# Decay columns for one more head pair, masks built on the core, and three moved steps in a fused attention and feed-forward kernel

## The chip, the core and the metric

The kernel runs on one core of a Trainium2 chip. The metric is the device time of one execution in microseconds (us). Seven runs of the kernel before gave a median of 367.82 us, from 362.78 to 372.94 us. One more execution was profiled: it took 362.79 us, of which 361.1 us lie between its first and its last instruction (the span). All times of single steps below come from that profiled execution and count from the start of its span.

## What is computed

Attention with a decay bias over 8 batches of 8 heads (576 positions, 64 numbers per head), followed by a feed-forward block with a hard-swish on the joined heads.

```python
scores = q @ k.T / sqrt(64)                       # per batch and head
cum    = cumsum(max(s, 0), axis=-1)
bias   = -(cum[:, None] - cum[None, :])
scores = where(upper triangle, -1e9, scores + min(bias, 0))
attn   = softmax(scores)
x      = (attn @ v), heads joined: 4608 x 512
h      = x @ w_in                                  # 512 -> 2048
out    = (h * clip(h + 3, 0, 6) / 6) @ w_out       # 2048 -> 512
```

## The kernel before

**Tiles.** The 64 heads are handled as 32 pairs. For a pair, q and k come from DRAM as f32 tiles of 128 positions (`qkf`), are cast to f16 by GpSimd, and are transposed by TensorE, so that the 64 head numbers lie on partitions 0 to 63 of a slot of `qkT` (three slots, used in turn: pair p lies in slot p % 3). Partitions 64 to 127 of a slot hold what is added to the scores by the same matmul: rows 64 to 67 the decay (for k the running sum in three f16 pieces, for q its negative, and ones opposite), rows 68 to 127 a coarse causal mask in steps of 10 positions. A score matmul over all 128 partitions so gives product, decay and mask at once. ScalarE takes the exponential into `Pm`, GpSimd clears the part above the diagonal (line 350), TensorE multiplies with `v` (line 425, `attend`), VectorE divides (lines 435 and 437), and a transpose puts the result into `xT`. The feed-forward block works on 9 blocks of 512 positions: `m1` (line 495) makes 16 pieces per block, each finished by ScalarE (line 505) and VectorE (line 506), and `m2` (line 540) makes the output.

**Four ways to put decay and mask into a slot.** Pairs 0 to 3 (`FIRST = 4`): the tile `x0` holds q or k cast to f16 together with 4 decay columns, which `first_columns` (line 742) makes with matmuls from a running sum over 64 positions each; `turn_first` (line 768 on) transposes q and k separately, 68 columns wide, and the eviction (line 781) writes rows 0 to 67. The mask rows of the three slots are copied once from a constant tile `amask` (`mask_part`, line 180; `mask_rows`, line 173). The fine mask is a third operand: a matmul of the identity `ident` with `tri`. Pairs 4 to 9: `transpose_group` (line 297) transposes q and k together; the decay rows come from DRAM, where `store_aug` put them after `decay_scan` and `decay_rows`, and `load_aug` reads them back. Pairs 10 to 31: one DMA transposes the tile `xb`, whose upper half holds the mask columns; these come from a constant in DRAM (`load_columns`, line 233), and GpSimd copies them into both buffers of `xb` (`copy_columns`, line 237).

**Order of work.** The order on each engine is that of the program text; nothing is moved by a scheduler. SyncE (SP) issues nearly all loads, in program order, and a load that has to wait holds up those behind it. GpSimd (POOL) issues the loads of `w_in` and `w_out` on a queue of their own (q0; SP's is q1). The stages are: a start (to some 9 us) in which TensorE runs filler matmuls on a zero tile (`keep_warm`); pairs 0 to 3 in halves of a head (to some 28 us); the first feed-forward block; pair 4 with pieces of it between; then `second_pair(p)` for pairs 5 to 8 (to some 75 us), in which one `m2` step is put in at fixed places; then `weave`, which spreads the attention of the remaining pairs among the `m1` and `m2` tasks by their weights. PSUM has eight banks: scores use the ring S (0, 1, 2), `m1` and `m2` mostly M (3, 4) and Y (5), the attention result 6 and 7.

Of the kernel before, what the change touches and what calls it, by code (L numbers as in the profile page):

```python
# [10 lines left out]
F16 = mybir.dt.float16  # L11
AF = mybir.ActivationFunctionType
ALU = mybir.AluOpType
# [3 lines left out]
def kernel(  # L17
# [10 lines left out]
    nc = tc.nc  # L28
# [40 lines left out]
    tri_np = np.where(np.arange(128)[None, :] < np.arange(128)[:, None], -65504.0, 0.0)  # L69
    idtri_dram = nc.inline_tensor(  # L70
        np.concatenate([np.eye(128), tri_np], axis=1).astype(np.float16), name="idtri"
    )

    NG = 72
    g = np.arange(NG)
# [13 lines left out]
    amask_np[1, 4:64] = np.where(gran[None, :] < rows[:, None], -16384.0, 0.0)  # L89
    MW = SEQ + 64  # L90
    amask_dram = nc.inline_tensor(
        np.ascontiguousarray(amask_np[:, :, np.arange(MW) % SEQ]), name="amask"
    )

    row = np.arange(W2).reshape(NTR, 128).T % SEQ
# [5 lines left out]

    FIRST = 4
    NA = 2 * (PTD - FIRST)
    aug_dram = nc.dram_tensor("aug_scratch", (2, 4, NA * SEQ), F16, kind="Internal").ap()
# [22 lines left out]
    XW = 68  # L127
    x0 = gT2[:, 1].rearrange("p f t -> p (f t)")[:, 0:FIRST * NTR * 2 * XW].rearrange(
        "p (a t i c) -> p a t i c", a=FIRST, t=NTR, i=2
    )  # L130

    amask = work.tile([128, 2, MW], F16, tag="amask", bufs=1)
    s_first = work.tile([NG, 64], F32, tag="s_first", bufs=1)
# [25 lines left out]

    nc.gpsimd.memset(warm, 0.0)  # L160
    nc.gpsimd.memset(x0[:, :, :, 0, D:D + 3], 1.0)
    nc.gpsimd.memset(x0[:, :, :, 1, D + 3:D + 4], 1.0)
    nc.gpsimd.memset(kT[:, :, W2:W2 + 64], 0.0)
    nc.gpsimd.memset(aug[:, 0, 0:3, :], 1.0)
    nc.gpsimd.memset(aug[:, 1, 3, :], 1.0)

    def more_pads():
        nc.gpsimd.memset(v_f[64:128, :, :, 4, :], 0.0)
        nc.gpsimd.memset(v_h[:, :, :, :, D:VW], 1.0)
        nc.gpsimd.memset(Pm[:, :, 1600:PW], 1.0)  # L170

    def mask_rows(sl, i, copy):
        copy(
            out=(kT, qT)[i][64:128, sl, 0:W2].rearrange("p (h t) -> p h t", h=2),
            in_=amask[64:128, i:i + 1, 0:SEQ].to_broadcast([64, 2, SEQ]),
        )

    def mask_part(sl, i, part, copy):
        c0, c1 = ((0, MW), (64, SEQ))[part]
        copy(  # L180
            out=(kT, qT)[i][64:128, sl, (0, MW)[part]:(MW, W2)[part]],
            in_=amask[64:128, i, c0:c1],
        )

# [32 lines left out]
    def load_aug(p, eng):  # L217
        sl = p % NS
        c0 = (p - FIRST) * W2
# [77 lines left out]
    def transpose_group(p, g):  # L297
        t0, t1 = ((0, 5), (5, 9))[g]
        n = (t1 - t0) * 128
        pT = f16(bank("S") if p == FIRST else PS[:, 3, :], n)  # L300
# [209 lines left out]
    def m1(n, f):  # L510
        if n == 0 and f < 8:
            ph = bank("A")
        elif n == 1 and f % 3 == 0:
            ph = bank("Y")
        elif n == 0 and f % 3 == 2:
            ph = bank("Y")
        elif n >= B - 1 and f % 2:
            ph = bank("S")
        else:
            ph = bank()  # L520
        m1_sum(n, f, ph, range(KC))
        m1_act(n, f, ph)
# [61 lines left out]
    def store_aug(eng):  # L584
        eng.dma_start(
            out=aug_dram.rearrange("i r (h t) -> h (i r) t", t=SEQ),
            in_=aug[2 * FIRST:2 * FIRST + NA].rearrange("h i r t -> h (i r) t"),
        )

    def load_pair(p):  # L590
        load_qk(p, nc.sync)
        load_v(p, nc.sync)
# [46 lines left out]
    def second_pair(p, fill):  # L639
# [6 lines left out]

        load_pair(p + 3)
        run(s0[:1])
        if first:
# [24 lines left out]
        if first:  # L674
            cast_qk(p + 1)
        cast_v(p + 1)
        if PTD <= p + 2:
            cast_columns(p + 2)
            transpose_dma(p + 2)
# [62 lines left out]
    def first_columns():  # L742
# [7 lines left out]
        for half in range(2):  # L750
# [7 lines left out]
            )  # L758
        c3 = cT.rearrange("p (a t) -> p a t", a=FIRST)
        r3 = rest.rearrange("p (a t) -> p a t", a=FIRST)  # L760
        hi, mid, lo = (x0[:, :, :, 1, D + j] for j in range(3))
# [23 lines left out]
    qk_tile(0)  # L785
    nc.sync.dma_start(out=s_first, in_=s[0].rearrange("h (c t) -> (h c) t", t=64))
    load_part(0, 0, 0, 5, A)
    A.dma_start(out=sums, in_=sums_dram.ap())
    load_part(0, 1, 0, 5, nc.sync)
    A.dma_start(out=idtri, in_=idtri_dram.ap())  # L790
    nc.sync.dma_start(out=amask[64:128], in_=amask_dram.ap().rearrange("i p t -> p i t"))
    load_part(0, 0, 5, 9, nc.sync)
# [8 lines left out]
    cast_first(0, 0, 0, 5, A.copy)  # L801
    cast_first(0, 1, 0, 5, G.tensor_copy)
    first_columns()
    mask_part(0, 1, 0, A.copy)
    mask_part(0, 0, 0, G.tensor_copy)
    keep_warm(4)
# [3 lines left out]
    cast_first(0, 1, 5, 9, G.tensor_copy)  # L810
    for i in range(2):
        mask_part(0, i, 1, V.tensor_copy)
    for i in range(2):
        mask_rows(1, i, V.tensor_copy)
    keep_warm(3)
    qk_f.pop(0)
    more_pads()
    for i in range(2):
        mask_rows(2, i, V.tensor_copy)

    def cast_pair(p):
        G.tensor_copy(out=x0[:, p, :, :, 0:D], in_=qk_f.pop(p))

    for hd in range(2 * FIRST):
        p, odd = hd // 2, hd % 2
        scores_half(hd, 0)
        if hd == 0:
            turn_first(0, 0, 5, 9, 6, V.tensor_copy)
            turn_first(0, 1, 5, 9, 7, V.tensor_copy)
        if not odd:  # L830
            if p == 0:
# [7 lines left out]
            if p == 1:  # L839
                nc.sync.dma_start(out=s_sb, in_=s.rearrange("b h t -> (b h) t"))  # L840
                load_v(3, nc.sync)
                load_qk(4, nc.sync)
            if p == 2:
                load_v(4, nc.sync)
                load_columns()
            if p == 3:
# [39 lines left out]
    m2_of = {n: m2_tasks(n) for n in range(NBLK)}  # L886
    run(transposes(FIRST))
    run(m1_0[10:12])
# [50 lines left out]
```

## Time and profile before

| | |
|---|---|
| median of 7 runs | 367.82 us |
| profiled execution, its span | 362.79 us, 361.1 us |
| TensorE (PE) busy | 350.6 us, 97% of the span |
| ScalarE (ACT), VectorE (DVE), GpSimd (POOL) busy | 209.0, 183.7, 152.7 us |
| clock granted to TensorE | 1.0 throughout |
| read from and written to DRAM | 37.54 MB, 9.55 MB |

The numbers are read as follows. A row of the timeline gives the start, the length, the engine (SPq and the like are the engines' queues of DMA issues), the line of the program, the operation and its tiles, how many instructions are merged, and in brackets the idle time before the row and what ended it. A row of waits gives who waited for whom, the sum, the number and the longest. A row of a DMA queue gives packets, megabytes and the share of the time of 16 DMA engines. PE is busy for 97% of the span, so what a change can take away from the end is mostly PE's idle time and PE's own work; a busy PE includes the filler matmuls of the start.

### The profile page before, as it was taken

What the parts mean: (1) busy time and instruction counts of PE and PEld (TensorE: products, weight loads), DVE (VectorE), ACT (ScalarE), POOL (GpSimd) and SP (SyncE); (2) the same over time, 40 slices, a digit from 0 to 9 for tenths busy, and PEclk for the clock granted to TensorE, in tenths of its full rate; (3) what the DMA queues carried; (4) which work ended last, traced back from release to release, by engine and by line L of the source; (5) the groups of instructions that cost most, each with busy time, mean ns of one, the idle gap of its engine ahead of it and who ended that gap; (6) DMA issues with size and microseconds to landing.
All of it is one profiled execution on the core that took longest, in us unless ns stands there. A gap on an engine that the chain in (4) does not pass through costs nothing.

```text
span 361.1 us, 7692 instructions
## 1 busy us (share of the span) xinstructions
PE 350.6 (97%) x2855; PEld 204.4 (57%) x2855; DVE 183.7 (51%) x309; ACT 209.0 (58%) x391; POOL 152.7 (42%) x375
## 2 busy tenths in 40 slices
PE   7899989999899999999999999999999999999996
PEld 3775546656555555555555555555555544544444
DVE  3776847656624554355535442545254636554431
ACT  3575637659936774677557764776477705543310
POOL 6659538755545454445544544555444200000000
PEclk9999999999999999999999999999999999999999
DMA  8999999999999899888988999999946110010012
GB/s 189 220 195 222 214 204 223 220 207 218 200 211 210 198 194 206 214 169 197 218 210 172 207 203 218 183 209 199 231 91 115 49 59 30 11 49 30 31 58 87
DMA packets 185586, 59.33 MB, mean 164 GB/s; under 512 B 177588, under 2 KB 180316, under 8 KB 185548
## 3 DMA queue, kind: packets, MB, share of 16 engines
q1 hardware_dynamic: 181832, 54.24, 67.2%
q0 software_dynamic: 2688, 4.19, 6.4%
q10 hardware_dynamic: 1028, 0.40, 0.4%
q8 instruction: 22, 0.36, 0.4%
q14 instruction: 16, 0.13, 0.1%
HBM read 37.54 MB, written 9.55 MB: 130 GB/s over the span
## 4 chain that ended last, share of the span: by engine, by line
PE 80%; DMA 6%; POOL 5%; ACT 3%; issue 2%; DVE 2%; SPq 0%; ACTq 0%; POOLq 0%; DVEq 0%
PE PS L540 31%; PE PS L495 29%; PE PS L337 8%; PE PS L425 6%; DMA qkf<-in_k_dram 4%; POOL t L227 2%; POOL Pm L350 1%; ACT Pm L345 1%; DMA aug_scratch<-aug 1%; PE PS L775 1%; PE PS L403 1%; ACT trl L505 1%; DVE gT L506 1%; PE PS L560 1%; DMA sums<-sums 1%
## 5 line engine op out<-in xcount | busy, mean ns | idle before, releaser
L506 DVE SCALAR_TENSOR_TENSOR gT<-trl,PS 128x512 f16<-128x512 f32 x144 | 98.2, 686 | 106.2 <-ACT trl L505 106.1
L495 PE MATMUL PS<-xT,w_in 128*128 128x512 f16 x576 | 143.7, 379 | 0.8 <-DVE gT L506 0.7
L505 ACT ACTIVATE trl<-PS,bias 128x512 f32<-128x512 f32 x144 | 99.0, 692 | 74.9 <-PE PS L495 73.0
L540 PE MATMUL PS<-w_out_sb,gT 128*128 128x512 f16 x560 | 138.5, 379 | 1.2 <-DVE gT L506 1.2
L345 ACT ACTIVATE Pm<-PS 128x384 f16<-128x384 f32 x224 | 103.1, 507 | 49.9 <-PE PS L337 48.6
L350 POOL TENSOR_SCALAR_AFFINE_SELECT Pm<-Pm 128x256 f16<-128x256 f16 x224 | 68.5, 307 | 118.2 <-ACT Pm L345 110.0
L495 PEld LDWEIGHTS <-w_in 128*128 128x128 f16 x576 | 61.3, 114 | 45.0 <-issue 2.0
L540 PEld LDWEIGHTS <-gT 128*128 128x128 f16 x560 | 51.4, 98 | 50.0 <-issue 1.7
L337 PE MATMUL PS<-qkT 128*128 128x256 f16 x392 | 63.2, 261 | 0.1
L337 PEld LDWEIGHTS <-qkT 128*128 128x128 f16 x392 | 36.2, 98 | 30.2 <-DVE qkT L308 1.2
L425 PEld LDWEIGHTS <-Pm 128*128 128x128 f16 x960 | 38.7, 97 | 10.9 <-DVE xs L437 0.7
L425 PE MATMUL PS<-v_h,Pm 128*128 128x65 f16 x960 | 41.9, 193 | 0.5 <-DVE xs L437 0.5
L549 DVE TENSOR_SCALAR osb<-PS 128x512 f32<-128x512 f32 x35 | 24.1, 688 | 32.9 <-PE PS L540 29.8
L437 DVE TENSOR_TENSOR xs<-PS,r 128x640 f16<-128x640 f32 x32 | 26.4, 825 | 1.1
L275 POOL CAST xb<-qkf 128x1152 f16<-128x1152 f32 x22 | 25.2, 1147 | 0.0
L290 POOL CAST v_h<-v_f 128x640 f16<-128x640 f32 x32 | 23.3, 729 | 1.5 <-DMA v_f<-in_v_dram 1.4
L409 ACT ACTIVATE Pm<-PS 128x896 f16<-128x896 f32 (+1 forms) x16 | 13.2, 836 | 5.7 <-PE PS L403 5.6
L308 DVE COPY qkT<-PS 64x640 f16<-64x640 f16 (+1 forms) x24 | 10.9, 454 | 9.2 <-PE PS L293 9.0
L435 DVE RECIPROCAL r<-PS 128x10 f32<-128x10 f32 x32 | 6.9, 216 | 8.0 <-PE PS L425 7.8
L403 PE MATMUL PS<-qkT 128*128 128x64 f16 (+4 forms) x48 | 9.6, 287 | 1.1 <-DVE qkT L781 1.0
L471 DVE COPY xT<-PS 128x576 f16<-128x576 f16 x14 | 6.4, 455 | 5.8 <-PE PS L463 4.5
L570 ACT ACTIVATE osb<-PS 128x256 f32<-128x256 f32 x1 | 0.4, 383 | 13.2 <-PE PS L560 13.2
(67 smaller groups left out, 126.0 us busy)
## 6 DMA issues: line engine op xcount, KB each, us to landing
out_dram<-osb SPq DMA_DIRECT2D x35, 256.0 KB, 2.3
qkf<-in_q_dram SPq DMA_DIRECT2D x31, 288.0 KB, 3.6
qkf<-in_k_dram SPq DMA_DIRECT2D x31, 288.0 KB, 3.7
v_f<-in_v_dram SPq DMA_DIRECT2D x64, 128.0 KB, 3.4
w_in<-in_moe_w_in_dram POOLq DMA_DIRECT2D x4, 512.0 KB, 12.6
w_out_sb<-in_moe_w_out_dram POOLq DMA_DIRECT2D x4, 512.0 KB, 13.4
v_f<-in_v_dram SPq DMA_DIRECT2D x32, 32.0 KB, 3.3
qkT<-xb SPq DMA_TRANSPOSE x22, 4.7
```

Of the source, the lines that this page charges most:

```text
L275: nc.gpsimd.tensor_copy(out=x.rearrange("p (i t) c -> p t i c", i=2)[:, :, :, 0:D], in_=qk_f.pop(p))
L290: nc.gpsimd.tensor_copy(out=v_h[:, sl, :, :, 0:D], in_=v_f[:, sl])
L337: nc.tensor.matmul(out=S[:, c:c + hi - lo], lhsT=kT[:, sl, off + 128 * kt:off + 128 * (kt + 1)], rhs=qT[:, sl, off + lo:off + hi], start=( ...
L345: nc.scalar.activation(out=P[:, p0:p0 + n], in_=S[:, 0:n], func=AF.Exp, scale=0.125, bias=0.0)
L350: nc.gpsimd.affine_select(out=view, in_=view, pattern=pattern, compare_op=ALU.is_ge, fill=0.0, base=0, channel_multiplier=-1,)
L425: nc.tensor.matmul(out=O[:, hh, qt * VW:qt * VW + D + 1], lhsT=P[:, c:c + 128], rhs=v_h[:, sl, hh, kt, 0:D + 1], start=(qt == 0), stop=(qt ...
L437: nc.vector.tensor_tensor(out=xs.rearrange("p t h d -> p h t d"), in0=Ov[:, :, :, 0:D], in1=r.to_broadcast([128, 2, 5, D]), op=ALU.mult,)
L495: nc.tensor.matmul(out=ph, lhsT=w_in_t[f // 4][:, kc, f % 4, :], rhs=xT[:, kc, n * 512:(n + 1) * 512], start=(kc == 0), stop=(kc == KC - 1),)
L505: nc.scalar.activation(out=trl, in_=ph, func=AF.Relu, bias=bias3[:, 0:1], scale=1.0)
L506: nc.vector.scalar_tensor_tensor(out=gT2[:, n % 2, f, :], in0=trl, scalar=6.0, in1=ph, op0=ALU.min, op1=ALU.mult)
L540: nc.tensor.matmul(out=po, lhsT=gT2[:, n % 2, f, t4 * 128:(t4 + 1) * 128], rhs=w_out_sb[:, f, :], start=(f == 0), stop=(f == NF - 1),)
L549: nc.vector.tensor_scalar_mul(out=osb, in0=po, scalar1=1.0 / 6.0)
```

## The change

Pair 4 is treated like pairs 0 to 3: its decay comes in columns (`COLS = 5`, so `first_columns` works on 90 instead of 72 groups of 64 positions), and its 9 double transposes become 18 single ones. Its decay rows are no longer stored and loaded. The constants `idtri` (64 KB) and `amask` (160 KB) are no longer loaded: VectorE fills `ident`, `tri` and the mask rows of slot 0 with a constant, and GpSimd cuts them to shape with six `affine_select` instructions. The mask rows of slots 1 and 2 are copied from slot 0 by VectorE, no longer ahead of the start of the scores but after the evictions of `turn_first` for heads 0 and 1. The k half of the first cast moves from GpSimd to ScalarE. `load_columns` (288 KB) moves from pair 2 to `second_pair(5)`, behind the load of pair 8, and `copy_columns` from pair 4 to the end of `second_pair(6)`. `load_aug` and `load_pair` change order for pair 6. Two fills for later tiles (`kT` pad, `aug` ones) move to later places on GpSimd. And the last of the 16 `m1` pieces of block 1 takes its bank from ring M instead of Y.

```diff
+    FIRST = 4
+    COLS = FIRST + 1
+    NG = COLS * W2 // 64
...
-    nc.gpsimd.memset(warm, 0.0)
+    def select(view, pattern, base, step, fill):
+        nc.gpsimd.affine_select(
+            out=view, in_=view, pattern=pattern, compare_op=ALU.is_ge, fill=fill,
+            base=base, channel_multiplier=step,
+        )
+
+    def mask_view(sl, i):
+        return (kT, qT)[i][64:128, sl, 0:W2].rearrange("p (h t) -> p h t", h=2)
+
+    nc.vector.memset(warm, 0.0)
+    nc.vector.memset(ident, 1.0)
+    nc.vector.memset(tri, 0.0)
+    nc.vector.memset(mask_view(0, 1), 0.0)
+    nc.vector.memset(mask_view(0, 0), 1.0)
+    select(ident, [[1, 128]], 0, -1, 0.0)
+    select(ident, [[-1, 128]], 0, 1, 0.0)
     nc.gpsimd.memset(x0[:, :, :, 0, D:D + 3], 1.0)
     nc.gpsimd.memset(x0[:, :, :, 1, D + 3:D + 4], 1.0)
-    nc.gpsimd.memset(kT[:, :, W2:W2 + 64], 0.0)
-    nc.gpsimd.memset(aug[:, 0, 0:3, :], 1.0)
-    nc.gpsimd.memset(aug[:, 1, 3, :], 1.0)
+    select(mask_view(0, 1), [[0, 2], [1, SEQ]], 4 * GRAN, -GRAN, -16384.0)
+    select(mask_view(0, 0), [[0, 2], [1, SEQ]], 4 * GRAN, -GRAN, 0.0)
+    select(mask_view(0, 0), [[0, 2], [-1, SEQ]], -4 * GRAN + GRAN - 1, GRAN, 0.0)
+    select(tri, [[1, 128]], 0, -1, -65504.0)
 
     def more_pads():
+        nc.gpsimd.memset(kT[:, :, W2:W2 + 64], 0.0)
...
-    def mask_rows(sl, i, copy):
...
+    def mask_rows(sl, i):
+        nc.vector.tensor_copy(out=mask_view(sl, i), in_=mask_view(0, i))
+
+    def aug_ones():
+        nc.gpsimd.memset(aug[:, 0, 0:3, :], 1.0)
+        nc.gpsimd.memset(aug[:, 1, 3, :], 1.0)
...
-        elif n == 1 and f % 3 == 0:
+        elif n == 1 and f % 3 == 0 and f + 1 < NF:
             ph = bank("Y")
...
         load_pair(p + 3)
+        if p == COLS:
+            load_columns()
...
         cast_v(p + 1)
+        if p == COLS + 1:
+            copy_columns()
...
-    A.dma_start(out=idtri, in_=idtri_dram.ap())
-    nc.sync.dma_start(out=amask[64:128], in_=amask_dram.ap().rearrange("i p t -> p i t"))
...
-    cast_first(0, 1, 0, 5, G.tensor_copy)
+    cast_first(0, 1, 0, 5, A.copy)
     first_columns()
-    mask_part(0, 1, 0, A.copy)
-    mask_part(0, 0, 0, G.tensor_copy)
...
-    for i in range(2):
-        mask_part(0, i, 1, V.tensor_copy)
-    for i in range(2):
-        mask_rows(1, i, V.tensor_copy)
     keep_warm(3)
     qk_f.pop(0)
     more_pads()
-    for i in range(2):
-        mask_rows(2, i, V.tensor_copy)
...
             turn_first(0, 0, 5, 9, 6, V.tensor_copy)
             turn_first(0, 1, 5, 9, 7, V.tensor_copy)
+        if hd < 2:
+            for i in range(2):
+                mask_rows(hd + 1, i)
...
             if p == 2:
                 load_v(4, nc.sync)
-                load_columns()
...
-    for p in range(FIRST, FIRST + 3):
-        if p > FIRST:
-            load_pair(p)
+    for p in range(COLS, COLS + 2):
         load_aug(p, nc.sync)
-    cast_qk(FIRST)
+        load_pair(p)
+    cast_pair(FIRST)
     cast_v(FIRST)
-    copy_columns()
...
-    run(transposes(FIRST))
+    for g, (t0, t1) in enumerate(((0, 5), (5, 9))):
+        for i in range(2):
+            turn_first(FIRST, i, t0, t1, (0, 1, 2, 7)[2 * g + i], V.tensor_copy)
```

More of the change, by code (lines that the diff above doesn't have):

```diff
@@ L67, in pair_of_banks @@
         return PS[:, b:b + 2, :].rearrange("p b c -> p (b c)")
[L69 to L74, printed above, removed]
+    FIRST = 4
+    COLS = FIRST + 1
+    NG = COLS * W2 // 64
     g = np.arange(NG)
@@ L89 @@
     amask_np[1, 4:64] = np.where(gran[None, :] < rows[:, None], -16384.0, 0.0)
[L90 to L93, printed above, removed]
     row = np.arange(W2).reshape(NTR, 128).T % SEQ
@@ L100 @@
     )
-    FIRST = 4
-    NA = 2 * (PTD - FIRST)
+    NA = 2 * (PTD - COLS)
     aug_dram = nc.dram_tensor("aug_scratch", (2, 4, NA * SEQ), F16, kind="Internal").ap()
@@ L127 @@
     XW = 68
-    x0 = gT2[:, 1].rearrange("p f t -> p (f t)")[:, 0:FIRST * NTR * 2 * XW].rearrange(
-        "p (a t i c) -> p a t i c", a=FIRST, t=NTR, i=2
+    x0 = gT2[:, 1].rearrange("p f t -> p (f t)")[:, 0:COLS * NTR * 2 * XW].rearrange(
+        "p (a t i c) -> p a t i c", a=COLS, t=NTR, i=2
     )
-    amask = work.tile([128, 2, MW], F16, tag="amask", bufs=1)
     s_first = work.tile([NG, 64], F32, tag="s_first", bufs=1)
@@ L170, in more_pads @@
         nc.gpsimd.memset(Pm[:, :, 1600:PW], 1.0)
-    def mask_rows(sl, i, copy):
[L173 to L183, printed above, removed]
+    def mask_rows(sl, i):
[3 more added lines that the diff above has]
+        nc.gpsimd.memset(aug[:, 1, 3, :], 1.0)
     qk_f = {}
@@ L218, in load_aug @@
         sl = p % NS
-        c0 = (p - FIRST) * W2
+        c0 = (p - COLS) * W2
         eng.dma_start(
@@ L299, in transpose_group @@
         n = (t1 - t0) * 128
-        pT = f16(bank("S") if p == FIRST else PS[:, 3, :], n)
+        pT = f16(PS[:, 3, :], n)
         src = qk_h[p]
@@ L586, in store_aug @@
             out=aug_dram.rearrange("i r (h t) -> h (i r) t", t=SEQ),
-            in_=aug[2 * FIRST:2 * FIRST + NA].rearrange("h i r t -> h (i r) t"),
+            in_=aug[2 * COLS:2 * COLS + NA].rearrange("h i r t -> h (i r) t"),
         )
@@ L758, in first_columns @@
             )
-        c3 = cT.rearrange("p (a t) -> p a t", a=FIRST)
-        r3 = rest.rearrange("p (a t) -> p a t", a=FIRST)
+        c3 = cT.rearrange("p (a t) -> p a t", a=COLS)
+        r3 = rest.rearrange("p (a t) -> p a t", a=COLS)
         hi, mid, lo = (x0[:, :, :, 1, D + j] for j in range(3))
@@ L785 @@
     qk_tile(0)
-    nc.sync.dma_start(out=s_first, in_=s[0].rearrange("h (c t) -> (h c) t", t=64))
+    nc.sync.dma_start(out=s_first, in_=s.rearrange("b h (c t) -> (b h c) t", t=64)[0:NG])
     load_part(0, 0, 0, 5, A)
@@ L842 @@
                 load_qk(4, nc.sync)
+                aug_ones()
             if p == 2:
                 load_v(4, nc.sync)
-                load_columns()
             if p == 3:
```

## The prediction

> **What bounds the kernel now.** I read the page first, for the share of each engine; then PE's waits over the whole span; then the timeline around each of them; last the DMA queues in windows of 5 us.
>
> ```profile
> PE 350.6 (97%) x2855; PEld 204.4 (57%) x2855; DVE 183.7 (51%) x309; ACT 209.0 (58%) x391; POOL 152.7 (42%) x375
> ```
>
> TensorE is the bound: 10.5 us of the span are left idle. PE's waits say where an edit can find some:
>
> ```profile
> PE PS L293 <- POOL t L227: 1.5, 4, 1.0
> PE PS L540 <- DVE gT L506: 1.2, 2, 1.0
> PE PS L403 <- DVE qkT L781: 1.0, 1, 1.0
> ```
>
> Three holes of 1.0 us each, and the change touches all three. The timeline shows their causes, in order of time:
>
> ```profile
> 11.19 0.97 DVE L173 COPY qkT<-amask 64x1152 f16<-64x1152 f16 x1
> 12.20 1.42 DVE L781 COPY qkT<-PS 68x512 f16<-68x512 f16 x3
> ...
> 50.30 1.14 POOL L227 CAST t<-qkf 128x1152 f16<-128x1152 f32 x1 [2.28 <-DMA qkf<-in_k_dram]
> 51.51 0.45 PE L293 MATMUL PS<-idtri,t 128*128 128x128 f16 x5 [1.02 <-POOL t L227]
> ...
> 98.50 0.69 DVE L506 SCALAR_TENSOR_TENSOR gT<-trl,PS 128x512 f16<-128x512 f32 x1 [0.59 <-ACT trl L505]
> 99.24 1.02 PE L540 MATMUL PS<-w_out_sb,gT 128*128 128x512 f16 x4 [1.00 <-DVE gT L506]
> ```
>
> At 12 us pair 0's second evictions stand behind mask copies. At 50 us pair 5's k comes late. At 99 us `m2` of block 1 wants bank 5, which `m1` piece 15 has just left.
>
> Why k is late (issued at 36.6, cast at 50.3) the queues between 35 and 40 us show, as packets, MB and share:
>
> ```profile
> q0 software_dynamic: 413, 1.04, 108.0%
> q1 hardware_dynamic: 43, 0.03, 2.6%
> ```
>
> The weights on q0 take the engines; SP's queue moves next to nothing until q0 ends at about 46 us.
>
> In the loop over pairs 5 to 8 (5.26 us each) PE has only 0.16 us of slack per pair, waiting for GpSimd:
>
> ```profile
> 64.13 0.72 POOL L290 CAST v_h<-v_f 128x640 f16<-128x640 f32 x1
> 64.96 0.41 POOL L350 TENSOR_SCALAR_AFFINE_SELECT Pm<-Pm 128x256 f16<-128x256 f16 x1
> 65.52 1.00 POOL L350 TENSOR_SCALAR_AFFINE_SELECT Pm<-Pm 128x128 f16<-128x128 f16 x3
> 66.47 1.14 POOL L227 CAST t<-qkf 128x1152 f16<-128x1152 f32 x1
> ...
> 67.67 0.45 PE L293 MATMUL PS<-idtri,t 128*128 128x128 f16 x5 [0.16 <-POOL t L227]
> ```
>
> Here GpSimd works without a gap worth naming from 64.13 to 68.41, and PE takes each result at once.
>
> **What the Trainium skill says.** "SBUF — State Buffer", section "Who interferes with whom": a VectorE copy in a two-port mode and a GpSimd instruction lock each other out for a whole instruction. The trace agrees: the four equal mask copies (line 173) took 0.45 to 1.39 us, and the 1.39 one ran beside GpSimd's cast of 9.23 to 10.59. "DMA: Bandwidth & Descriptors", section "Queues, rings and completion order": each engine takes packets from its queues in turn; with the large weight packets on q0 that fits the starved q1 above.
>
> **The change part by part.**
>
> *Start, to 9.3 us.* The path is: k lands (5.24), its cast (0.45), the decay column on ScalarE (5.72, 0.33), four VectorE steps to 7.36, k's transposes to 8.22, three fillers, scores. The k cast moves to ScalarE, where q's took 0.46: nothing. Without two loads of 224 KB, k may land some 0.2 us sooner. Against that VectorE gets five memsets before the running sum. No row shows one of any size; "VectorE: DVE Perf Modes", section "Zero memsets can be issued as uint32 (trn2)", gives one cycle per element, and the page's clock is 0.96 GHz: estimated 0.53 + 0.13 + 0.13 + 2 x 1.2 = 3.2 us, half of the zero parts less if issued as uint32. With 0.06 each (the bias memset) VectorE is free at 3.6 to 4.4 instead of 2.78; scale and scan (0.91 to scan's end) put the sum at 4.5 to 5.3 and the matmuls (0.65) at 5.2 to 6.0, against ScalarE's start at 5.72. So -0.2 to +0.3; I take 0. The selects: 128x128 takes 0.29, 128x256 0.41, so 0.9 ns an element; 1152 elements 1.2 us; three of these and three of 0.29 end at about 7.0, before GpSimd's next casts (7.57) and before k's eviction (8.31). Covered; were they twice as slow, some 2 us would come out. The kT fill (0.38) puts the cast of pair 1 at 9.6: its transposes are wanted at 10.75, ready at about 10.8: nothing.
>
> *Mask copies behind the evictions.* Pair 0's evictions (2 x 0.42) now end at about 11.4, so the hole of 1.0 goes. But before, four copies (3.23 us) ran from 8.94 on while VectorE had nothing else; now it is idle then and does them between evictions that PE waits for: evictions to 11.4, two copies, pair 1's q (0.75), k's transposes wait for that since they share banks 4 and 5, two copies, pair 1's k (0.75), and only then the scores of head 2, which started at 15.18. With copies of 0.45 that is 14.7 (-0.5), with 0.81, the mean now, 16.1 (+0.9), with all at 1.39 18.5 (+3.3). GpSimd has casts for some 2.6 of these 4 us, so two of four are locked out: I take +0.4. From there to 26 us PE was full, so it stays.
>
> *Pair 4 in columns.* 18 narrow transposes of 0.055 (9 in 0.50) for 9 of 0.05: +0.5 PE, before the hole at 50 us. The casts and evictions are as many as before. SP still waits for the store of the decay rows (landed 35.71) before pair 5's loads: no gain from the removed load.
>
> *Pair 5's k.* `xaug` (288 KB) was issued at 21.79, so it shared the engines with `w_in`. At the 220 KB per us of these windows its absence lets q0 end 1.3 us sooner, and k with it. The early 224 KB I count at nothing: at 15 to 20 us the engines were at 0.89, so SP's issues were the limit. Without waiting PE would arrive at 50.48 + 0.5 + 0.4 = 51.4, the cast ends at 51.45 - 1.3 = 50.15: the hole of 1.0 is gone, but 0.9 of it is filled by what went before. Net at this point: +0.4 + 0.5 - 1.0 = -0.1.
>
> *Column copies in the loop.* Two copies of 1.18 (line 237), at 34.25 hidden by `m1`, now follow the cast of v at 64.85. Behind them stand head 14's four selects, the cast of pair 8 and head 15's selects. The selects end at 68.4 instead of 66.5 and the cast at 69.6 instead of 67.6, so transposes of pair 8 start at about 69.6 instead of 67.67: +1.95, and PE has no slack up to 98 us to get it back. The copy also waits for the table: it is issued behind pair 8's v, which ended at 62.68, or some 1.3 sooner with q0; its own issue takes 0.71 and loads of this size land 3.8 after issue, so 65.1 to 66.5 against 64.85. I take +0.4 (0 to 1.6).
>
> *Bank of `m1` piece 15.* Ring M gives it the bank of piece 13, whose reader on VectorE ended at 96.46; PE wants it at 96.44. `m2` then finds bank 5 free since piece 12 (95.7). The wait of 1.0 goes: -1.0 (0 if its first matmuls meet another wait).
>
> Sum: -0.1 + 1.95 + 0.4 - 1.0 = **+1.25 us**, so a span of 362.4 for 361.1, or +0.35%. The profiled execution is 5 us below the median; I scale the median: 367.82 x 1.0035 = **369.1 us**. That is no change that can be measured: the seven runs spread over 10 us, and I take 1% (3.7 us) as what can be told from none.
>
> **The rivals.**
>
> *R1, slower: the table comes late in the loop.* Each us that `xaug` lands after 64.85 costs PE one more, as all of GpSimd stands behind the copy. SP issues without a gap from 49.5 to 75 us, so its queue is full, which speaks for it; landings there took 3.7 to 4.1 us, which speaks against. It decides from a landing at about 67.6 on (-0.1 + 1.95 + 2.8 - 1.0 = +3.65); at 68.5 it gives 361.1 + 4.5 = 365.6, median 372.4.
>
> *R2: the copies lock out.* All four mask copies at 1.39 us: +2.9 over my sum, with nothing to absorb it, since the hole at 50 us is filled already: 365.3, median 372.1. Against it: GpSimd waits for loads of pairs 2 and 3 (1.0 and 1.8 us) in that time.
>
> *R3, faster: the lighter DMA counts for more than in this execution.* The median lies 5 us above the profile. If what lengthens those runs is the load-bound stretch to 55 us, the 0.5 MB less (2.4 us at 220 KB per us) count in full and k's hole there is longer than 1.0: up to -4, median about 364. The one trace shows no such run, so this stays a guess.
>
> *R4: it doesn't do what it says.* GpSimd's copies fit into its gaps (1.1 us per pair): they would cost 0.9 in place of 2.35, so the sum is -0.2, and with unlocked mask copies -1.1: 360.0 to 360.9, median 366.7 to 367.6. Against it: the gaps are waits for exponentials, which come after.
>
> **How the numbers follow.** My sum 0.52, R1 0.12, R2 0.08, R3 0.13, R4 0.15. R4 and mine lie within 1%; the spread of a median of few runs (about 1.5 us) takes some out on either side: within 1% 0.60, faster 0.17, slower 0.23. Low end: R4's lower end less 2.2 for the spread and part of R3, 364.5; high end: R1 and R2, 373. My own case alone, from unlocked mask copies (0.9 less) to copies of 0.81 and a table at 66.5 (1.7 more), spans 368.2 to 370.8.
>
> **What would show it.** Right: the PE wait for line 781 near 12 us gone, but a new one of VectorE before head 2; no PE wait for line 227 at 50 us; the two column copies at 65 us with pair 8's transposes 2 us later than pair 7's rhythm of 5.26; no wait at `m2` of block 1. Wrong: mask copies of 0.45 throughout, or selects of the start that end after 8.3, or a copy that waits for `xaug` beyond 66.5. A PE total that grows by much more than 0.5 would mean work that I have not counted.

## The result and the profile after

24 runs of the changed kernel gave a median of 365.65 us (363.00 to 368.23), beside 368.13 us (361.97 to 373.71, 59 runs) for the kernel before. The ratio of times is 1.0064, with a 95% interval of 1.0039 to 1.0088: no change by the bound of 1%, though the interval leaves out 1. This ratio is of undisturbed runs, those within 1.5% of the fastest of each kernel; over all runs the medians stand the other way round, because the kernel before has more long runs. The profiled execution took 364.96 us with a span of 363.3, so 2.2 us more than before, where +1.25 was forecast. Its granted clock was 0.994 on the mean.

The page of the changed kernel says that TensorE is the bound as before, with about as much work (349.9 us for 350.6) and more idle time (13.4 us of the span for 10.5):

```profile
PE 349.9 (96%) x2864; PEld 204.6 (56%) x2864; DVE 184.5 (51%) x312; ACT 208.8 (57%) x391; POOL 156.0 (43%) x378
```

PE's waits over the whole span of the changed kernel (who waited for whom, sum, times, longest):

```profile
PE PS L426 <- POOL Pm L351: 2.3, 2, 1.9
...
PE PS L294 <- POOL t L228: 1.0, 3, 0.7
PE PS L780 <- DVE qkT L786: 1.0, 1, 1.0
...
PE PS L404 <- DVE qkT L786: 0.6, 1, 0.6
...
PE PS L541 <- DVE gT L507: 0.2, 1, 0.2
```

Of the three holes of before, the one at `m2` is gone (1.2 before, 0.2 now, line 541) and so is the 1.0 for GpSimd's cast at 50 us. The one for the evictions at 12 us is replaced by two, at 13.48 and 15.65 (lines 780 and 404). A new one of 1.9 us heads the list: TensorE waits for GpSimd's mask. The timeline of the changed kernel shows the places, in order of time:

```profile
3.82 1.17 DVE L751 TENSOR_TENSOR_SCAN scan<-s_first 90x64 f32<-90x64 f32 x1
...
11.74 0.83 DVE L180 COPY qkT<-qkT 64x1152 f16<-64x1152 f16 x2
12.68 0.75 DVE L786 COPY qkT<-PS 68x1152 f16<-68x1152 f16 x1
13.46 1.35 DVE L180 COPY qkT<-qkT 64x1152 f16<-64x1152 f16 x2
...
15.65 0.39 PE L404 MATMUL PS<-qkT 128*128 128x512 f16 x1 [0.59 <-DVE qkT L786]
...
30.85 0.33 SPq L586 DMA_DIRECT2D aug_scratch<-aug  x1
40.08 0.27 SPq L221 DMA_DIRECT2D qkT<-aug_scratch  x1
...
50.37 1.15 POOL L228 CAST t<-qkf 128x1152 f16<-128x1152 f32 x1 [1.37 <-DMA qkf<-in_k_dram]
...
62.48 0.45 PE L294 MATMUL PS<-idtri,t 128*128 128x128 f16 x5 [0.16 <-POOL t L228]
...
66.36 2.24 POOL L238 COPY xb<-xaug 128x1152 f16<-128x1152 f16 x2 [1.44 <-DMA xaug<-xaug]
68.55 1.10 POOL L351 TENSOR_SCALAR_AFFINE_SELECT Pm<-Pm 128x256 f16<-128x256 f16 x4
69.01 0.33 PE L426 MATMUL PS<-v_h,Pm 128*128 128x65 f16 x5 [1.90 <-POOL Pm L351]
...
70.81 0.45 PE L294 MATMUL PS<-idtri,t 128*128 128x128 f16 x5 [0.73 <-POOL t L228]
...
101.22 1.02 PE L541 MATMUL PS<-w_out_sb,gT 128*128 128x512 f16 x4
```

The row at 66.36 is the centre of it. GpSimd was idle for 1.44 us until the table (`xaug`) had landed, then copied for 2.24 us; only then did the selects follow that PE was waiting for. Pair 8's transposes start at 70.81, 8.33 us after pair 7's, where the rhythm before was 5.26. The matmul at 101.22 has no bracket: the wait of before is gone.

The windows of 1 us of the changed kernel (stretch, length, busy time of PE, PEld, DVE, ACT, POOL, then granted clock, DMA share, GB/s) show why the mean clock is below 1:

```profile
7.00:8.00 1.00, 0.53 (x6) 0.56 (x7) 0.64 (x2) 0.00 (x0) 0.55 (x2) 0.65 1.30 243
8.00:9.00 1.00, 1.00 (x5) 0.28 (x3) 0.00 (x0) 0.69 (x1) 0.89 (x4) 0.50 0.78 176
9.00:10.00 1.00, 1.00 (x6) 0.57 (x5) 0.00 (x0) 0.00 (x0) 1.00 (x3) 0.50 1.15 261
```

For 3.4 us at the start of the scores, from 7.3 to 10.7, the clock was halved. The kernel before had 1.0 throughout its profiled execution.

### The profile page after: what moved, and what is told of

It is laid out like the page before. It is cut to its first block, busy times and chain, and to the rows that moved or that the text cites. A ratio compares the mean times of both kernels' runs of the same rounds, so it can differ in the third digit from the quotient of the medians.

```text
span 363.3 us, 7714 instructions
## 1 busy us (share of the span) xinstructions
PE 349.9 (96%) x2864; PEld 204.6 (56%) x2864; DVE 184.5 (51%) x312; ACT 208.8 (57%) x391; POOL 156.0 (43%) x378
## 4 chain that ended last, share of the span: by engine, by line
PE 83%; DVE 5%; POOL 4%; DMA 3%; ACT 2%; issue 2%; SPq 0%; POOLq 0%; DVEq 0%; ACTq 0%
PE PS L496 32%; PE PS L541 31%; PE PS L338 9%; PE PS L426 6%; DMA qkf<-in_k_dram 3%; POOL Pm L351 1%; POOL t L228 1%; PE PS L404 1%; PE PS L561 1%; ACT trl L506 1%; DVE gT L507 1%; PE PS L780 1%; PE PS L464 1%; ACT Pm L346 1%; POOL xb L238 1%
## 5 line engine op out<-in xcount | busy, mean ns | idle before, releaser
L541 PEld LDWEIGHTS <-gT 128*128 128x128 f16 x560 | 51.4, 98 | 48.8 <-issue 0.5
L426 PEld LDWEIGHTS <-Pm 128*128 128x128 f16 x960 | 38.7, 97 | 13.4 <-POOL Pm L351 2.6
L309 DVE COPY qkT<-PS 64x640 f16<-64x640 f16 (+1 forms) x20 | 9.1, 455 | 11.3 <-PE PS L294 11.1
L786 DVE COPY qkT<-PS 68x1152 f16<-68x1152 f16 (+2 forms) x13 | 7.3, 587 | 5.4 <-PE PS L780 5.3
```

The costliest lines, as they stand in the source:

```text
L426: nc.tensor.matmul(out=O[:, hh, qt * VW:qt * VW + D + 1], lhsT=P[:, c:c + 128], rhs=v_h[:, sl, hh, kt, 0:D + 1], start=(qt == 0), stop=(qt ...
L541: nc.tensor.matmul(out=po, lhsT=gT2[:, n % 2, f, t4 * 128:(t4 + 1) * 128], rhs=w_out_sb[:, f, :], start=(f == 0), stop=(f == NF - 1),)
```

## The experiments

Three sets of runs, each on one chip with runs of the kernel before beside them; the changed kernel itself ran again in the second set only (a1). Medians in us, lowest and highest in brackets, number of runs; the ratio to before with its 95% interval where it was taken.

| run | median | span | ratio |
|---|---|---|---|
| e1_table_early | 362.94 (362.70 to 365.07), 4 | 361.0 | |
| e2_columns_early | 361.76 (361.05 to 364.61), 5 | 362.9 | |
| e3_bank_back | 366.79 (364.78 to 368.37), 4 | 363.1 | |
| e4_masks_early | 364.83 (364.24 to 366.75), 4 | 365.0 | |
| before, first set | 368.91, 7 | | |
| a1_after_again | 366.90 (365.23 to 370.17), 6 | 364.5 | 1.0012 (0.9918 to 1.0106) |
| b1_masks_split | 362.03 (361.88 to 365.08), 6 | 360.5 | 0.9887 (0.9807 to 0.9967) |
| b2_split_k_ahead | 363.28 (363.05 to 363.79), 6 | 361.3 | 0.9909 (0.9845 to 0.9974) |
| b3_pair4_rows | 363.88 (361.70 to 364.98), 6 | 363.2 | 0.9914 (0.9836 to 0.9992) |
| before, second set | 370.84, 11 | | |
| c1_ones_later | 361.84 (361.34 to 369.80), 17 | 360.3 | 0.9965 (0.9948 to 0.9982) |
| c2_ones_later_rows | 365.57 (360.11 to 371.94), 22 | 369.8 | 0.9944 (0.9903 to 0.9984) |
| c3_ones_later_split | 361.93 (361.13 to 370.91), 22 | 360.0 | 0.9976 (0.9961 to 0.9991) |
| c4_before_bank | 367.29 (360.38 to 372.16), 22 | 360.4 | 0.9979 (0.9950 to 1.0009) |
| before, third set | 367.37, 70 | | |

The kernel before spreads over more than 10 us, and so do c2 and c4; a ratio from few runs hangs on which of its runs fell into that set. Kernels are therefore compared with their neighbours of the same set where there are any, and by the rows of their traces, one profiled execution for each.

**e1_table_early: the late table undone, the late copies kept.**

```diff
-        if p == COLS:
-            load_columns()
...
             if p == 2:
                 load_v(4, nc.sync)
+                load_columns()
```

> The changed kernel with only the load of the mask-column table back at pair 2; the copies stay at the end of the step for pair 6. Theory A (late table): the copies start at 64.9 instead of 66.4, pair 8's transposes at 69.4 instead of 70.8, and the span falls from 363.3 by 1.4 to 361.9, if pair 5's k still lands by 50.4. Theory B (the table's absence from the early queue is what keeps k at 50.4): k lands about 1.3 us later, the cast of pair 5 starts at 51.7, PE waits 1.3 us for it, and the span stays at 363.2.

The span was 361.0, so 2.3 less than with the whole change. The timeline of this run, GpSimd and PE in the loop:

```profile
61.73 0.45 PE L294 MATMUL PS<-idtri,t 128*128 128x128 f16 x5 [0.16 <-POOL t L228]
...
64.11 2.24 POOL L238 COPY xb<-xaug 128x1152 f16<-128x1152 f16 x2
66.30 1.10 POOL L351 TENSOR_SCALAR_AFFINE_SELECT Pm<-Pm 128x256 f16<-128x256 f16 x4
...
68.55 0.45 PE L294 MATMUL PS<-idtri,t 128*128 128x128 f16 x5 [0.73 <-POOL t L228]
```

The copies start with no wait and take 2.24 us, as in the changed kernel. Pair 8 follows pair 7 after 6.82 us, for 8.33 with the table late and 5.26 in the rhythm. So the late table is worth 1.51 us and the copies in the loop 1.56. The other 0.75 us of the gain was there ahead of the loop (61.73 for 62.48). Of it, 0.44 us was there already at head 2 (15.21 for 15.65), near the start, where the changed kernel's profile had its clock at half. The remaining 0.3 us came at pair 5's k, which was cast at 49.31 for 50.37, though the table was loaded early; so its early load is not what made that k late. Theory A, the table as a separate cost, holds; theory B, a later k and no gain, does not.

**e2_columns_early: table and copies both at their old places.** On top of e1's edit:

```diff
-        if p == COLS + 1:
-            copy_columns()
...
     cast_v(FIRST)
+    copy_columns()
```

> The changed kernel with the table's load back at pair 2 and the column copies back behind the first cast of v for pair 4. Theory A (the loop's copies are the loss): no PE wait for the select of line 351 near 69 us, the four steps of the loop keep their rhythm of 5.26 us, span 363.3 - 3.1 = 360.2, that is below the kernel before by the bank's 1.0. Theory B (k is then late): the hole at 50 us is back with 1.3 us, span 361.5.

The rhythm of 5.26 us came back (65.21, 70.47, 75.73 for pairs 7, 8 and 9). Four of five runs lie at 361.05 to 362.27, with spans of 359.3 to 360.6, as theory A had it (360.2). The profiled one was the fifth, 364.61, and its timeline shows at another place what cost it 3 us:

```profile
14.03 1.53 POOL L183 MEMSET aug<- 64x1728 f16 x1
14.39 3.46 DVE L180 COPY qkT<-qkT 64x1152 f16<-64x1152 f16 x2
...
15.50 0.89 POOL L184 MEMSET aug<- 64x576 f16 x1
16.34 1.13 POOL L812 CAST gT<-qkf 128x1152 f16<-128x1152 f32 x1
...
18.69 0.39 PE L404 MATMUL PS<-qkT 128*128 128x512 f16 x1 [2.70 <-DVE qkT L782]
```

The second pair of mask copies took 3.46 us for 0.83 elsewhere. It lasted as long as GpSimd ran one instruction after another, two fills and a cast, and PE waited 2.7 us for the eviction behind it. This is rival R2 of the prediction, with GpSimd's moved fills (`aug`) as a part of what locks VectorE out. The start of this kernel is that of the changed kernel, where the same pairs of copies took 0.83 and 1.35 us in the first profile, and no pair more than 1.76 in the profiles of e1, e3 and a1. There the second pair began ahead of the fills (12.9 to 13.5); here it began at 14.39, as the first pair had taken 1.78 us beside a cast.

**e3_bank_back: piece 15 of block 1 again on ring Y.**

```diff
-        elif n == 1 and f % 3 == 0 and f + 1 < NF:
+        elif n == 1 and f % 3 == 0:
```

> The changed kernel with piece 15 of block 1 back on ring Y. Theory A: a PE wait of 1.0 us at the first m2 step of block 1 (near 101 us), span 364.3. Rival: the later and shifted loop has spread the work of ScalarE and VectorE so that piece 15's readers are no longer late, no wait, span 363.3.

The timeline of this run has the wait again:

```profile
101.05 1.02 PE L541 MATMUL PS<-w_out_sb,gT 128*128 128x512 f16 x4 [1.00 <-DVE gT L507]
```

So the bank edit is worth 1.0 us at this place. The span (363.1) didn't grow to theory A's 364.3, as two other things were shorter in this execution: PE reached pair 5 at 50.99 for 51.57, half of that from the start and half from k (cast at 48.65, without a wait for DMA), and GpSimd's wait for the table was 0.72 for 1.44.

**e4_masks_early: the four mask copies ahead of pair 0's second evictions.**

```diff
+    for sl in (1, 2):
+        for i in (1, 0):
+            mask_rows(sl, i)
     for hd in range(2 * FIRST):
...
-        if hd < 2:
-            for i in range(2):
-                mask_rows(hd + 1, i)
```

> The changed kernel with the four mask copies ahead of the second evictions of pair 0, in the place they had in the kernel before (their source is slot 0 as in the changed kernel). Theory A (the copies cost 0.5 us between the evictions, but what is won before 50 us is lost in the wait for pair 5's k): head 2's scores start at about 14.9 instead of 15.65, the PE wait for line 228 near 50 us grows by about as much, span 363.2. Theory C (the early shift goes through to the end): span 362.6. Rival D (with the copies ahead the hole at 12 us of the kernel before comes back in full): head 2 at 15.2 and a wait of 1.0 for the second evictions.

The timeline of this run:

```profile
8.69 3.47 DVE L180 COPY qkT<-qkT 64x1152 f16<-64x1152 f16 x4
12.19 1.42 DVE L786 COPY qkT<-PS 68x512 f16<-68x512 f16 x3
...
13.00 0.39 PE L404 MATMUL PS<-qkT 128*128 128x512 f16 x1 [0.82 <-ACT Pm L410]
```

The evictions stand behind the copies again, and the hole of before is back (0.82). (The row names ScalarE, which ended its exponential at 12.98, at about the same time as the second eviction.) Yet head 2's scores start at 15.17, as early as before (15.18). The changed kernel had 15.65 in its profiled execution, but 15.21, 15.37 and 15.53 in e1, e3 and a1, which have the same order here at full clock. The place of the mask copies moves the wait and is worth 0 to 0.4 us. Rival D had that; theory A's 14.9 fell. The span of 365.0 comes from the loop: GpSimd waits 1.70 us for the table there, PE 2.15 us for GpSimd, followed by a clock of 0.58 and 0.56 in the windows 68:72 and 72:76.

**a1_after_again: the changed kernel, unaltered, in the second set.**

> The changed kernel once more, beside the next three. Theory A (the loop's copies and the late table): again a PE wait near 68 us for the selects of line 351, of 1.2 to 2.2 us according to when the table lands (65.0 to 66.4), and span 362.5 to 363.5 where no stretch runs at a granted clock of 0.5. If TensorE's long waits are what lets its clock be halved, a stretch at 0.5 lies next to one of the waits (the start, or 67 to 76 us), and nowhere else.

Its span was 364.5. PE waited 1.96 us for GpSimd in the loop, and the windows of 4 us of this run show what came then:

```profile
68.00:72.00 4.00, 2.26 (x24) 1.66 (x25) 0.79 (x2) 0.49 (x1) 3.18 (x9) 0.80 0.88 220
72.00:76.00 4.00, 4.00 (x36) 2.35 (x35) 1.90 (x5) 2.20 (x5) 2.04 (x6) 0.77 1.12 236
```

PE was busy 2.26 of 4 us, with a clock of 0.80 and then 0.77: up to 0.20 x 4 + 0.23 x 4 = 1.7 us lost on top of the wait. The stretch at half clock lies next to a wait, as expected. k was cast at 48.82 in this run, 1.55 sooner than in the first profile, and did not wait for DMA.

**b1_masks_split and b2_split_k_ahead: on top of e2, another place for the copies, and pair 5's loads sooner.** b1 puts slot 1's copies ahead of the first scores and slot 2's behind pair 1's eviction; b2 also issues pair 5's q and k in pair 2, ahead of the store of the decay rows.

```diff
+    for i in (1, 0):
+        mask_rows(1, i)
     for hd in range(2 * FIRST):
...
-        if hd < 2:
-            for i in range(2):
-                mask_rows(hd + 1, i)
...
             turn_first(p + 1, 1, 0, 9, 4, V.tensor_copy)
+            if hd == 1:
+                for i in (1, 0):
+                    mask_rows(2, i)
             if p + 2 < FIRST:
                 cast_pair(p + 2)
```

```diff
             if p == 2:
...
                 load_columns()
+                load_qk(5, nc.sync)
...
     for p in range(COLS, COLS + 2):
         load_aug(p, nc.sync)
-        load_pair(p)
+        if p > COLS:
+            load_qk(p, nc.sync)
+        load_v(p, nc.sync)
```

> Table and column copies early, as in the second experiment; slot 1's mask copies ahead of pair 0's second evictions, slot 2's behind the eviction of pair 1's k. Head 2's scores at 14.3 instead of 15.2 to 15.65. Theory A (pair 5's k sets the time at 50 us): the PE wait there grows by as much, and the span equals that of the second experiment's usual executions (359.7). Theory C (the shift goes through): 358.8.

> As the run with the mask copies split, and the loads of pair 5's q and k issued at pair 2 behind the column table, ahead of the store of the decay rows instead of behind it. Theory A: the cast of pair 5 does not wait for k, no PE wait near 50 us, and the 0.9 us won at the start comes through: span 358.8. Rival (the small packets on SP's queue delay the store and the weights instead): a wait for the decay rows or for v of pair 5 near 52 us, span 359.7 or more.

In b1 slot 2's copies fell under GpSimd's fills again (3.64 us at 14.03), and PE waited 1.9 us. The median of 362.03 is that of e2 within its spread, and the five runs at full clock have spans of 360.2 to 360.5: theory C's 358.8 fell. In b2 the timeline shows pair 5's k on SP's queue and its cast:

```profile
25.52 6.57 SPq L195 DMA_DIRECT2D qkf<-in_k_dram  x1
32.20 14.08 SPq L586 DMA_DIRECT2D aug_scratch<-aug  x1
49.66 0.27 SPq L221 DMA_DIRECT2D qkT<-aug_scratch  x1
...
49.87 1.14 POOL L228 CAST t<-qkf 128x1152 f16<-128x1152 f32 x1 [0.64 <-DMA qkf<-in_k_dram]
```

k was issued at 25.5 and still landed only at 49.9: 24 us, while the weights were on q0. Issued at 40.8 in the changed kernel, it landed at 50.4. Theory A fell: the cast still waited 0.64 us for k. The issue of the store behind it took 14 us, and pair 5's v came 2.68 us late, as the rival had it, though PE didn't wait for either. What PE waited for is the pair after: 1.26 us at 58.32 for the cast of pair 6, whose k was issued behind all this (at 52.96, for 50.92 in b1). The median is 1.2 us above b1's. The two landings suggest that k hangs on the weights and not on SP's order; no run here moves the weights.

**b3_pair4_rows: on top of e2, pair 4 with rows from DRAM again.**

```diff
-    COLS = FIRST + 1
+    COLS = FIRST
...
-    cast_pair(FIRST)
+    cast_qk(FIRST)
...
-    for g, (t0, t1) in enumerate(((0, 5), (5, 9))):
-        for i in range(2):
-            turn_first(FIRST, i, t0, t1, (0, 1, 2, 7)[2 * g + i], V.tensor_copy)
+    run(transposes(FIRST))
```

> Table and column copies early, as in the second experiment, and pair 4 undone: its decay comes as rows from DRAM, its transposes are double, the sum works on 72 groups. Theory A (columns for pair 4 cost 0.5 of PE and save nothing): PE arrives 0.5 sooner at pair 5's transposes, but waits for k, which lands as before: span 359.7, same as the second experiment. Rival (the change's point: without the rows of pair 4 something waits less): the scores of pair 4 wait for the decay rows near 42 us when the store lands late (40 us in the changed kernel), span 361 or more.

Inconclusive for pair 4: the first pair of mask copies was locked out for 4.07 us here, and PE waited 4.21 us at 16.60, which is more than the edit itself could be worth. The median is 1.9 us above b1's. What the run does show is how far the lock-out can go: one copy alone took 2.98 us.

**c1_ones_later: on top of e2, GpSimd's `aug` fills from pair 1 to pair 3,** so that they no longer stand among the mask copies.

```diff
                 load_qk(4, nc.sync)
-                aug_ones()
...
             if p == 3:
+                aug_ones()
                 decay_scan()
```

> As the second experiment (table and column copies early), and the two fills of the decay tile with ones moved from pair 1 to pair 3 on GpSimd. Theory E (mask copies of VectorE are locked out by GpSimd's run of a cast, two fills and a cast at 13 to 17.5 us): each pair of copies takes at most 1.8 us, head 2's scores at 15.2 to 15.7 instead of 18.7, span 359.5 in the profiled execution too. Rival (the copies lose to the casts as well): a pair of copies above 3 us again.

The timeline of this run:

```profile
11.73 1.77 DVE L180 COPY qkT<-qkT 64x1152 f16<-64x1152 f16 x2
...
14.40 0.83 DVE L180 COPY qkT<-qkT 64x1152 f16<-64x1152 f16 x2
...
15.69 1.15 POOL L812 CAST gT<-qkf 128x1152 f16<-128x1152 f32 x1 [1.60 <-DMA qkf<-in_k_dram]
```

With the fills gone GpSimd is idle for 1.6 us, and the second pair of copies takes 0.83 for 3.46. That is theory E, that the fills are a part of what locks the copies out, as far as one profile of each version can show it. The first pair still took 1.77 us beside a cast, and head 2's scores came at 16.07, later than the 15.2 to 15.7 expected, with a halved clock at the start as in the changed kernel. 15 of 17 runs lie at 361.34 to 362.16. c1 is a steady version: 0.9965 (0.9948 to 0.9982) of before, a gain below the 1% of the prediction, but with an interval that leaves out 1. Its 361.84 lies well below the 365.65 and 366.90 of the changed kernel, though those are of other sets.

**c2_ones_later_rows and c3_ones_later_split: c1 with b3's edit, and c1 with b1's split of the mask copies.** The diffs are those of b3 and b1.

> As the run with the ones moved to pair 3, and pair 4 with rows from DRAM. Theory A: columns for pair 4 cost PE 0.5 that the wait for pair 5's k takes up: same time as with columns, within 0.3 us. Rival: rows cost time, as the scores of pair 4 wait for a store that lands late: slower by 1 us or more. Third: 0.5 faster, if k lands before PE comes.

> As the run with the ones moved to pair 3, and the mask copies split: slot 1's ahead of pair 0's second evictions, slot 2's behind the eviction of pair 1's k. Head 2's scores at 14.3. Theory A (k of pair 5 sets the time at 50 us): no more than 0.3 us below the run with the ones moved alone. Theory C: 0.9 below.

c3 has the median of c1 (361.93 for 361.84), as theory A had it, but not for its reason. Head 2's scores came at 14.06, 2.0 us sooner than in c1. Of this, 1.3 us was lost at 27 us, to another lock-out:

```profile
22.54 1.58 POOL L183 MEMSET aug<- 64x1728 f16 x1
...
23.23 1.72 DVE L134 TENSOR_SCALAR s<-s_sb 64x576 f32<-64x576 f32 x1
...
27.36 0.65 PE L426 MATMUL PS<-v_h,Pm 128*128 128x65 f16 x15 [1.74 <-DVE xs L438]
```

The moved fills now stand beside the first step of `decay_scan` (line 134), which took 1.72 us for 0.44 in c1, where it began after them. PE then waited 1.74 us for VectorE (0.46 in c1). Pair 5's k came late again (its cast waited 1.28 us and ended at 51.35), but PE reached that point at about the same time: its transposes start at 51.41, for 51.70 in c1.

c2's shortest runs lie below c1's: the median of the 9 runs with a granted clock of 0.998 and more is 361.05, for 361.82 of 12 such runs of c1. So pair 4's columns cost some 0.8 us where the rows come in time; the prediction had 0.5 for the transposes. But 11 of c2's 22 runs took over 366 us, and 2 of c1's 17, so that over all runs c2's median is 3.7 us higher. The rival is right for the long runs, the third case for the short ones; theory A, no difference, fell. The one execution of c2 that was profiled is a long one (371.5 us); its first row of PE's waits is

```profile
PE PS L338 <- DMA qkT<-aug_scratch: 8.9, 1, 8.9
```

Pair 4's scores waited 8.9 us for the decay rows, which were still on their way through DRAM: the store was issued at 30.43, the load that reads it back only at 48.85.

**c4_before_bank: the kernel before with the bank edit of e3 alone, in the other direction.**

```diff
-        elif n == 1 and f % 3 == 0:
+        elif n == 1 and f % 3 == 0 and f + 1 < NF:
```

> The kernel before with only the bank of piece 15 changed. Expected: the PE wait of 1.0 near 99 us gone and nothing else, so a span of 360.1 for 361.1 where the clock is granted in full. Rival: the wait moves to the next step of m2 or to ScalarE: 361.1.

The wait at `m2` is gone here too, and the shortest runs gain: with a clock of 0.998 and more the median is 362.09, for 362.76 of 22 such runs of before in this set. These are five runs, and the ratio of 0.9979 (0.9950 to 1.0009) doesn't tell the kernel from no change. Its profiled execution, one of the short ones (362.09 us), has as PE's longest wait

```profile
PE PS L337 <- DMA qkT<-aug_scratch: 1.9, 1, 1.9
```

so the wait of c2 comes, shorter, in the old form of pair 4 in an ordinary execution too, which the profiled execution of before happens not to have.

## Why the prediction was right, and where it was not

The forecast of no change by 1% was right, and so were its mechanism and most of its terms. The bound is wide, though: the ratio of 1.0064 and the medians, which lie 0.67% the other way, both count as no change. The span came out at 363.3 for 362.4. By steps:

- **Start, 0 forecast: right.** Head 0's scores start at 9.26 for 9.29 before (9.42 to 9.55 in a1, e1 and e3). The sum was inside its bounds (ready at 5.0), for another reason than the memsets alone: the scan took 1.17 us for 0.29 before, beside GpSimd's selects. These took 1.16 us each (1.2 estimated) and ended at 6.4.
- **Mask copies, +0.4: the measured +0.47 agrees in part by luck.** Head 2 started at 15.65 for 15.18, but the same order started it at 15.21, 15.37 and 15.53 in e1, e3 and a1, so the edit is worth 0 to 0.4. The clock at half in the profiled execution may have added the rest; that isn't shown. That GpSimd's casts slow a part of the copies was right (1.35 us for the second pair, 0.83 for the first). The lock-out, rival R2, got 8% and turned up in four later profiles (e2, b1, b2 and b3: 3.30 to 4.07 us for a pair), where the copies met the moved `aug` fills; of the five profiles with the changed kernel's own start (its first, a1, e1, e2, e3) only e2 shows it. The prediction counted the casts there but not those fills.
- **Pair 4 in columns, +0.5 on PE: right.** The 18 narrow transposes took 1.19 us, the 9 double ones 0.68; by the runs it is some 0.8 (c2 against c1). PE's total doesn't show it, as PE was busy for 5.96 of the first 9 us in place of 7.16. **"No gain from the removed load": wrong in general.** It was read from one execution in which the store came in time. c4 shows a wait of 1.9 us for it and c2 one of 8.9.
- **Pair 5's k 1.3 us sooner: right in a1 and e3, wrong in the profiled execution.** Those two cast it 1.48 and 1.65 sooner than before (48.82 and 48.65 for 50.30). The reason given is borne out in part: between 44 and 48 us q0 moved 0.45 MB before, 0.18 in a1 and 0.08 in e3. But e1, with the table early, had k 1.0 sooner too. In the profiled execution q0 was down to 0.22 MB as well, and k was as late as ever. The store of the decay rows was answered late there, 9.2 us after its issue (30.85 to 40.08) for 5.4 before (30.42 to 35.86), but that isn't enough to explain it: in e1 the same took 11.4 us (30.40 to 41.84). Why k was late stays open. The hole went all the same: PE reached that point at 51.45, 51.4 being forecast.
- **Column copies in the loop, +2.35: the term that was mis-sized, at +3.07.** The copies had +1.95 and cost 1.56 (e1). The late table had +0.4 and cost 1.51, close to the upper bound of 1.6. The table landed at 66.36, at the end of the 65.1 to 66.5 given; the value taken should have been nearer that end, since the SP queue was known to be full. In the other profiles with the table late it landed at 65.04 (e3), 65.84 (e4) and 66.00 (a1), and GpSimd waited 0.72 to 1.70 us for it. A later table was R1, and at 67.6 it would have decided.
- **Bank, -1.0: right to the digit** in the traces (e3, and the rows of line 541).

The sum by these terms: 0.47 + the net of pair 4 and k (-0.41, so +0.06 at pair 5) + 3.07 - 1.0 = +2.1, for +2.2 measured. Where no halved clock comes in, the change may cost less: the median of the 5 runs of the changed kernel with 0.998 and more is 364.08, against 362.76 for such runs of before in the third set, +1.3. That is a hint only, as the five spread from 363.00 to 368.21 and the sets differ.

One thing was not in the forecast at all, the clock. The Trainium skill, "TensorE: Matmul & The Clock Gate", section "What's actually happening", says that the array's clock is halved after an idle window of some 3.4 us, and that the window runs freely. The traces agree on the half (0.50) and on the chance in it: the same kernel had its dip at 8 us in one execution and at 70 us in another. All six dips (the changed kernel, a1, e4, b3, c1, c2) lie beside waits of PE. In two profiles PE was idle for that long: in c2 the clock fell 3.6 us into the wait of 8.9, and in b3 just behind the wait of 4.2. In the others it was not: in the 3.4 us ahead of the fall PE was busy for 0.70 us in a1, 1.26 in e4 and 1.78 in the changed kernel. So the runs show the fall after a window that was only in part idle, and not how much idle time it takes; the first profile of the changed kernel had the wait of 1.9 us in the loop without a dip behind it.

**The predicted median of 369.1 was 3.5 us too high,** though inside its range. The prediction saw that the median of before lay 5 us above the profiled execution, didn't explain it, and scaled it. Of the kernel before, 26 of 59 runs took more than 369 us, of the changed kernel's 24 none. Rival R3 named that case, called it a guess, and gave 364. It has some support as to the place, the stretch up to 55 us bound by loads, but it counted the bytes and k, where two profiles show pair 4's decay rows. Kernels with these rows spread over 10 us (before, c4, c2), c1 and c3 have 3 of 39 runs above 366, and c2 differs from c1 in pair 4 alone. But that the wait for the decay rows makes the long runs is read from two profiles; b3's six runs, with rows, show none above 365, and of the changed kernel's, without them, 11 of 24 lie above 366. It is likely, not shown.

A rival is the clock: of the 36 runs of before above 366 us in the third set none had a granted clock above 0.995. The two come together, and in the one profile that shows both, c2's, the wait is the larger: PE began to wait at 42.0, and of the time at half clock (45.6 to 55.8) it worked for 5.0 us, so up to 2.5 us were lost to the clock beside the 8.9 of the wait. What also stays open is how much of the changed kernel's own spread (363 to 368) is clock and how much the late table, since only profiled executions tell where the time went; its five runs at full clock spread as far as the rest.

## What to carry to other kernels

Moved work costs what the engine at its new place has to spare: 2.24 us of copies were free under a feed-forward block, and held PE up by 1.56 us in a loop with 0.16 us of slack per turn, by 3.07 with their input late. A load that such work needs should stay early, even if it seems to crowd the start: e1 loads it early and loses nothing there (k cast at 49.31, for 48.65 to 50.37 in the four profiles with the table late). And before scaling a median that lies 5 us above the profiled execution, ask which wait comes only sometimes; an edit that removes such a wait may show nothing in the one trace.

## What the runs showed of the hardware

- The Trainium skill, "SBUF — State Buffer", section "Who interferes with whom", has the lock-out of VectorE and GpSimd by whole instructions. The runs go further than the prediction took from it: two VectorE copies (0.83 us in all when GpSimd was idle) took 3.30 to 4.07 us beside back-to-back fills and casts on GpSimd (b2, e2, b1, b3), a single one 2.05 us in e2 and 2.98 in b3. So one lock-out after another can be lost, and fills that only write take part: beside them alone the first step of `decay_scan` took 1.72 us for 0.44 (c3, c1).
- Pair 5's k on SP's queue, issued 15 us sooner beside the weights (25.5 in b2 for 40.8), landed half a microsecond sooner (49.9 for 50.4 in the changed kernel's first profile). Between 42 and 44 us of the kernel before, q0 and q1 moved 109 packets each, of 0.39 and 0.03 MB in all: packet for packet, the queue with the small ones moves little.
- Fills with zero on VectorE went out at half the count of elements: 64x576 as uint32 in 0.54 us, for 1.02 of 64x1152 ones.
- The clock of 0.50 came for 3.4 us at a time in the changed kernel, a1, b3 and c1, for 6.8 us in e4 and 10.2 in c2: once, twice and three times the same length.
